# Feed-forward block on one core: the first chunk of x by DMA transposes instead of PE transposes

## Chip, cores and metric

The kernel runs on 1 core of one Trainium2 chip. The metric is the device time of one execution in microseconds (us), the median of several. The kernel before takes 94.9 us. All tensors are bf16, sums are fp32.

The profile names the engines PE (TensorE matmul), PEld (TensorE weight load), DVE (VectorE), ACT (ScalarE), POOL (GpSimd) and SP (SyncE). A name with a q (ACTq, SPq) is an engine's sequencer issuing DMAs. The granted clock is the share of TensorE's full clock that the profile says it was given. A DMA is issued by an engine, and it lands when its data has arrived and the semaphore says so; times of both are counted from the start of the profiled span.

## The reference

```python
# x: 1 x 2048 x 448, w1: 448 x 1792, w2: 1792 x 448
h = jnp.einsum("bsd,df->bsf", x, w1) + b1
h = gelu(h)                      # tanh approximation
return jnp.einsum("bsf,fd->bsd", h, w2) + b2
```

## The kernel before

The tokens are worked in four chunks of 512. Layer 1 needs x transposed (columns of x on the partitions, tokens along the row); 448 columns make three slots of 128 and one of 64. Each matmul uses 64 rows of the array where the dummy matmuls use 128 (forms 64\*128 and 128\*128 in the profile), and two of them, on the two row halves, run side by side: in the trace they start 3 to 4 ns apart. Such a pair is the unit of time: with 512 tokens the next one starts about 0.216 us later, and a chunk's layer 1 is 49 such pairs, 10.6 us. Two blocks of 128 hidden columns make an item, which holds one of four PSUM units.

How the first chunk gets in and is transposed:

```python
load_x()          # SyncE queue: xn[128 partitions, 4 tiles, 448], plain load, 448 KB
load_w1(0)        # 384 KB: hidden columns of items 0 and 1
load_w1r()        # 224 KB: the last 64 rows of w1
load_w1(1)        # 384 KB: items 2 and 3
load_w1(2)        # 576 KB
load_w2(0, 7); load_w2(7, 14); b2 ...          # 784 KB each
for c in range(1, NSC):                        # chunks 1 to 3: DMA transposes
    for slot, d0 in enumerate((0, P, 2 * P, D - P)):
        ... xT[:, slot, c*SC:(c+1)*SC] <- x2[c*SC:(c+1)*SC, d0:d0+P], transpose=True
# ... cut ...
warm(NWARM)       # 7 dummy matmuls of 512 columns, 0.43 us apart
for t, copier in enumerate(("vector", "scalar", "vector", "scalar")):
    ... turn(t, copier)       # PE transposes of one tile into PSUM, then one copy into xT
for c in range(NSC):
    items = [layer1(c, j) for j in range(2)]
    if c == 0:
        turn_b1() ...
        for t0 in (0, HC):                     # first half of the tokens, then the second
            for item in items:
                item[0](t0, t0 + HC)
    # ... cut: the other items, then layer 2 of the chunk ...
```

In layer 2 of the last chunk the last tile (`last=True`) adds its bias by a matmul, just before that tile's own matmuls:

```python
def part_a():
    need = free(u)                             # gelus that still read this PSUM unit
    if last:
        pr.op("tensor", ... matmul(unit[u][:, 1, 0:n], ones, b2_z ...), after=need + ["b2z"])
    # ... cut ...
```

Of the kernel before, what the change touches and what calls it, by code (L numbers as in the profile page):

```python
# [10 lines left out]

class Program:

# [3 lines left out]
    def __init__(self, nc, es):  # L17
        self.nc, self.es = nc, es
        self.lists = {e: [] for e in self.COMPUTE + ("sync",)}
        self.sems = {e: es.enter_context(nc.semaphore(f"sem_{e}")) for e in self.COMPUTE}  # L20
        self.count = dict.fromkeys(self.COMPUTE, 0)
        self.where = {}

    def op(self, engine, make, after=(), event=None):
        if event is not None:
            self.count[engine] += 1
            self.where[event] = (f"sem_{engine}", self.sems[engine], self.count[engine])
        self.lists[engine].append((make, tuple(after), self.sems[engine] if event else None, 1))

    def dma(self, engine, make, event, after=()):  # L30
        if event not in self.where:
            name = "dma_" + "_".join(str(p) for p in (event if isinstance(event, tuple) else (event,)))
            self.where[event] = (name, self.es.enter_context(self.nc.semaphore(name)), 0)
        name, sem, n = self.where[event]
        self.where[event] = (name, sem, n + 16)
        self.lists[engine].append((make, tuple(after), sem, 16))

    def barrier(self, engine, after):
        self.lists[engine].append((None, tuple(after), None, 0))

    def emit(self):
        for name in self.lists:
            self._run(getattr(self.nc, name), name)

    def _run(self, eng, name):
        seen = {}
        for make, after, sem, inc in self.lists[name]:
            for event in after:
                key, s, value = self.where[event]
                if seen.get(key, 0) < value:  # L50
                    eng.wait_ge(s, value)
                    seen[key] = value
            if make is None:
                continue
            done = make(eng)
            if sem is not None:
                done.then_inc(sem, inc)


def bass_standalone__dense_activation_gelu__prompt_kernel(  # L60
# [21 lines left out]
    NWARM = 7  # L82

    with ExitStack() as es:
# [5 lines left out]
        xn = sb("xn", [P, STC, D], BF16)  # L90
        xr = sb("xr", [P, STC, P], BF16)
        ident = sb("ident", [P, P], BF16)
        junk = sb("junk", [P, 1], BF16)
        b1n = sb("b1n", [P, P], BF16)
        b1_f = sb("b1_f", [P, NFT], FP32)
        b2_bc = sb("b2_bc", [P, D], BF16)
        g = sb("g", [P, NFT, S], BF16)
# [8 lines left out]
        x0v = x2[0:SC, :].rearrange("(p t) d -> p t d", t=STC)  # L106
        o0v = out2[0:SC, :].rearrange("(p t) d -> p t d", t=STC)


        W1CUTS = (0, 4, 8, 14)  # L110

        def load_x():
            pr.dma("sync", lambda e: e.dma_start(xn[:, :, :], x0v[:, :, :]), "x")  # L113
# [16 lines left out]
        load_x()  # L130
# [6 lines left out]
        pr.dma("sync", lambda e: e.dma_start(b2_bc[:, :], b2.partition_broadcast(P)), "b2")  # L137
        for c in range(1, NSC):
            for slot, d0 in enumerate((0, P, 2 * P, D - P)):
                pr.dma("sync", lambda e, c=c, slot=slot, d0=d0: e.dma_start(  # L140
                    xT[:, slot, c * SC:(c + 1) * SC], x2[c * SC:(c + 1) * SC, d0:d0 + P], transpose=True), ("xT", c))


        pr.op("gpsimd", lambda e: e.memset(ident[:, :], 0.0), event="ident0")
        pr.op("gpsimd", lambda e: e.affine_select(
            out=ident[:, :], in_=ident[:, :], compare_op=ALU.not_equal, fill=1.0,
            base=0, pattern=[[-1, P]], channel_multiplier=1), after=["ident0"], event="ident")
        pr.op("vector", lambda e: e.memset(b1n[:, :], 0.0), event="b1z")  # L148
        pr.dma("scalar", lambda e: e.dma_start(b1n[0:NFT, :], b1.rearrange("(c p) -> c p", p=P)), "b1n",
               after=["b1z"])  # L150
        pr.op("scalar", lambda e: e.activation(junk[:, :], one, ACT.Gelu_apprx_tanh))  # L151


        busy = {}
# [6 lines left out]
        def stage(t):  # L161
            return unit[t // 2][:, t % 2, 0:2 * P].bitcast(BF16)

        def twice(t):
            pr.op("vector", lambda e: e.tensor_copy(  # L165
                xr[:, t, :].rearrange("p (two h) -> p two h", two=2),
                xn[:, t, D3:D].unsqueeze(1).broadcast_to([P, 2, H])), after=["x"], event=("xr", t))

        def turn(t, copier):
            for k in range(KT + 1):  # L170
                src = xn[:, t, k * P:(k + 1) * P] if k < KT else xr[:, t, :]
                need = ["ident", "x"] if k < KT else [("xr", t)]
                pr.op("tensor", lambda e, k=k, src=src: e.transpose(  # L173
                    stage(t)[:, k * P:(k + 1) * P], src, ident[:, :]),
                    after=need, event=("xt", t) if k == KT else None)

            def evac(e):
                o = xT[:, :, t * P:(t + 1) * P]
                i = stage(t).rearrange("p (k s) -> p k s", k=KT + 1)
                return e.copy(o, i) if copier == "scalar" else e.tensor_copy(o, i)  # L180

            pr.op(copier, evac, after=[("xt", t)], event=("xT0", t))
            busy[(t // 2, t % 2)] = ("xT0", t)

        def turn_b1():
            b1T = unit[0][:, 1, 0:H].bitcast(BF16)
            pr.op("tensor", lambda e: e.transpose(b1T, b1n[:, :], ident[:, :]),
                  after=["b1n", "ident", ("xT0", 1)], event="b1T")
            pr.op("vector", lambda e: e.tensor_copy(b1_f[:, :], b1T[:, 0:NFT]), after=["b1T"], event="b1")
            busy[(0, 1)] = "b1"  # L190




        order = [2]
# [9 lines left out]
        serial = [0]  # L205

        def fence():
            serial[0] += 1
            return ("half", serial[0])

        def layer1(c, j):
            u = next_unit()
            c0, c1 = c * SC, (c + 1) * SC
            turned = fence()

            def mm(lo, half, k, t0, t1, first, fin, after, event):
                ft = 2 * j + lo
                rows = slice(half * H, (half + 1) * H)
                lhsT = w1_sb[rows, k, ft * P:(ft + 1) * P] if k < KT else w1r[rows, ft * P:(ft + 1) * P]
                pr.op("tensor", lambda e: e.matmul(  # L220
                    unit[u][:, lo, t0:t1], lhsT=lhsT, rhs=xT[rows, k, c0 + t0:c0 + t1], start=first, stop=fin,
                    skip_group_check=c == 0 and j < 2), after=after, event=event)

            def part_a(t0=0, t1=SC):

                need = free(u) if t0 == 0 else []
                need += [("xT0", t) for t in range(t0 // P, t1 // P)] if c == 0 else [("xT", c), ("xTd", c)]
                for k in range(KT):
                    for lo in (0, 1):
                        after = (need if k == 0 else []) + [("w1", w1_of(2 * j + lo))]  # L230
                        mm(lo, lo, k, t0, t1, k == 0 and t0 == 0, False, after,
                           turned if k == KT - 1 and lo and t1 == SC else None)

            def part_b():
                for k in range(KT + 1):
                    for lo in (0, 1):
                        fin = k == KT
                        mm(lo, 1 - lo, k, 0, SC, False, fin, [turned] if k == 0 else ["w1r", "w1rU"] if fin else [],
                           ("h", c, 2 * j + lo) if fin else None)
                for lo in (0, 1):  # L240
                    ft = 2 * j + lo
                    pr.op("scalar", lambda e, lo=lo, ft=ft: e.activation(  # L242
                        g[:, ft, c0:c1], unit[u][:, lo, :], ACT.Gelu_apprx_tanh,
# [3 lines left out]
            return part_a, part_b  # L247

        def store(c, st, after):
            j = c * STC + st  # L250
            dst = o0v[:, st, :] if c == 0 else out2[j * P:(j + 1) * P, :]
            pr.dma("sync", lambda e: e.dma_start(dst, out_sb[:, j, :]), "out", after=after)

        def layer2(c, tiles, last=False):

            u = next_unit()
            split = len(tiles) == 1
            n = DH if split else D
            turned = fence()

            def mm(ft, lo, half, first, fin, after, event):
                st = tiles[0] if split else tiles[lo]
                j = c * STC + st
                rows = slice(half * H, (half + 1) * H)
# [135 lines left out]
```

## Time and profile before

| | kernel before |
|---|---|
| median of 4 runs | 94.88 us (94.75 to 95.02) |
| profiled span | 93.5 us |
| PE busy | 90.2 us, 97% of the span |
| granted clock | 1.00 |
| first layer-1 matmul | 6.23 us |
| first layer-2 matmul | 16.83 us |

First, the chain of waits of the kernel before, followed back from its last instruction. Columns: start, length (us), what it was.

```profile
1.19 5.00 DMA w_sb<-in_w_dram
...
6.23 10.77 PE u L220 x110
17.00 10.59 PE u L266 x112
...
80.50 6.73 PE u L266 x85
...
```

One wait of 5 us for w1's first piece, then only matmuls to the end: L220 is layer 1, L266 layer 2. The first chunk's layer 1 (10.77) is hardly longer than a later one (10.58), so all that a better start can save lies before 6.23 us.

Second, the timeline of its start. Columns: start, length, engine, line, operation, out<-in, form, count, and in brackets the idle time before it and what ended it.

```profile
0.73 0.40 SPq L113 DMA_DIRECT2D xn<-in_x_dram  x1
1.19 0.42 SPq L120 DMA_DIRECT2D w_sb<-in_w_dram  x1
...
3.91 0.30 DVE L165 COPY xr<-xn 128x128 bf16<-128x128 bf16 x2 [2.98 <-DMA xn<-in_x_dram]
...
5.98 0.59 ACT L180 COPY xT<-u 128x512 bf16<-128x512 bf16 x1 [0.33 <-PE u L173]
...
6.23 2.13 PE L220 MATMUL u<-xT,w_sb 64*128 64x256 bf16 x30 [0.17 <-DMA w_sb<-in_w_dram]
```

x has landed by 3.9 us and is transposed and copied by 6.6; w1's first piece lands at 6.2. The two paths end nearly together.

Third, what the view of the tile xT says of the DMA transposes of chunks 1 to 3: issue time as min/median/max in ns, then the time from issue to landing.

```profile
L140 SPq DMA_TRANSPOSE xT<-in_x_dram x12: 1251/1262/2087, 9.2 to 25.5; - x12
...
DMA to landing us min/median/max: 3.0/4.0/6.0
```

All twelve have the same size, 512 tokens by 128 columns.

Fourth, the timeline where layer 1 of the last chunk ends:

```profile
79.68 2.42 ACT L242 ACTIVATE g<-u,b_f 128x512 bf16<-128x512 f32 x4 [0.24 <-PE u L220]
...
80.13 0.38 PE L220 MATMUL u<-xT,w1r 64*128 64x512 bf16 x2
...
80.34 6.89 PE L266 MATMUL u<-w_sb,g 64*128 64x448 bf16 x85
```

Layer 2 starts at 80.34 without a pause, while the last four gelus run until 82.1.

### The profile page before, as it was taken

The numbers are of one execution on the slowest core, as the hardware profiler recorded it, in microseconds if no ns is written. First come the engines' busy times: TensorE is split into PE (matmuls) and PEld (weight loads), VectorE is DVE, ScalarE is ACT, GpSimd is POOL, SyncE is SP. The second block draws the span as 40 slices with busy tenths as digits, with TensorE's granted clock in tenths as the row PEclk, the third lists the DMA queues.
The fourth block names the chain that finished last, engine by engine and source line by source line (L and its number), as shares of the span: only waits on it lengthen the run. The fifth ranks groups of instructions, "written<-read, shape, count | busy, mean of one in ns | idle before, by whom it ended". The sixth has DMA issues, their size and how long they took to land.

```text
span 93.5 us, 2049 instructions
## 1 busy us (share of the span) xinstructions
PE 90.2 (97%) x933; PEld 46.7 (50%) x933; DVE 12.3 (13%) x29; ACT 38.0 (41%) x61; POOL 1.1 (1%) x7
## 2 busy tenths in 40 slices
PE   6999999999999999999999999999999999999990
PEld 2475444555454444455554444455554444475890
DVE  0151001100334000000234000000134000000421
ACT  3353787900002887900001878900001878910001
POOL 4000000000000000000000000000000000000000
PEclk9999999999999999999999999999999999999999
DMA  2999999745665000000033000000033000000023
GB/s 51 324 224 365 379 328 126 136 94 113 64 128 173 0 0 0 7 0 0 0 102 101 0 0 0 4 7 0 0 98 98 0 7 0 0 0 7 17 81 98
DMA packets 12260, 7.32 MB, mean 78 GB/s; under 512 B 6940, under 2 KB 12060, under 8 KB 12252
## 3 DMA queue, kind: packets, MB, share of 16 engines
q1 hardware_dynamic: 12224, 7.20, 31.3%
q8 instruction: 7, 0.11, 0.5%
q10 hardware_dynamic: 28, 0.00, 0.0%
q14 instruction: 1, 0.01, 0.0%
HBM read 3.79 MB, written 1.84 MB: 60 GB/s over the span
## 4 chain that ended last, share of the span: by engine, by line
PE 91%; DMA 5%; SPq 0%; DVE 0%; issue 0%
PE u L266 46%; PE u L220 45%; DMA w_sb<-in_w_dram 5%; SPq L113 0%; DVE out_sb L305 0%; PE u L273 0%
## 5 line engine op out<-in xcount | busy, mean ns | idle before, releaser
L242 ACT ACTIVATE g<-u,b_f 128x512 bf16<-128x512 f32 x56 | 35.0, 686 | 40.5 <-PE u L220 40.5
L266 PE MATMUL u<-w_sb,g 64*128 64x448 bf16 (+1 forms) x504 | 43.2, 328 | 0.0
L220 PE MATMUL u<-xT,w_sb 64*128 64x512 bf16 (+1 forms) x348 | 40.9, 369 | 0.2 <-DMA w_sb<-in_w_dram 0.2
L266 PEld LDWEIGHTS u<-w_sb,g 64*128 64x128 bf16 x504 | 24.5, 94 | 18.4
L220 PEld LDWEIGHTS u<-xT,w_sb 64*128 64x128 bf16 x348 | 16.9, 94 | 19.3 <-DMA w_sb<-in_w_dram 0.5
L290 DVE TENSOR_TENSOR out_sb<-u,b_bc 128x448 bf16<-128x448 f32 x14 | 8.1, 620 | 61.2 <-PE u L266 61.2
L220 PE MATMUL u<-xT,w1r 64*128 64x512 bf16 x56 | 10.6, 376 | 0.0
L220 PEld LDWEIGHTS u<-xT,w1r 64*128 64x128 bf16 x56 | 2.7, 94 | 3.3
L308 ACT CAST out_sb<-u 128x224 bf16<-128x224 f32 x1 | 0.3, 346 | 9.2 <-PE u L266 9.2
L158 PE MATMUL u<-const-bfloat16-1.0 128*128 128x512 bf16 x7 | 3.1, 627 | 0.8 <-PEq L385 0.8
L180 ACT COPY xT<-u 128x512 bf16<-128x512 bf16 x2 | 1.2, 586 | 2.3 <-PE u L173 2.3
L158 PEld LDWEIGHTS u<-const-bfloat16-1.0 128*128 128x128 bf16 x7 | 0.9, 137 | 2.1 <-issue 2.1
L151 ACT ACT_TABLE_LOAD x1 | 1.3, 1283 | 1.6 <-DVE b1n L148 1.6
L173 PE MATMUL u<-ident,xn 128*128 128x128 bf16 x12 | 1.8, 308 | 0.1
L173 PEld LDWEIGHTS u<-ident,xn 128*128 128x128 bf16 x12 | 1.3, 138 | 1.0 <-issue 1.0
L361 DVE COPY xT<-xT 64x512 bf16<-64x512 bf16 x3 | 0.9, 289 | 3.5 <-DMA xT<-in_x_dram 3.4
L173 PE MATMUL u<-ident,xr 128*128 128x128 bf16 x4 | 1.2, 306 | 0.0
L357 DVE COPY b_z<-b_bc 1x448 bf16<-1x448 bf16 x1 | 0.3, 267 | 6.5 <-DMA b_bc<-in_b_dram 6.5
L165 DVE COPY xr<-xn 128x128 bf16<-128x128 bf16 x4 | 0.6, 190 | 3.0 <-DMA xn<-in_x_dram 3.0
L180 DVE COPY xT<-u 128x512 bf16<-128x512 bf16 x2 | 0.9, 426 | 0.7 <-PE u L173 0.7
L298 DVE TENSOR_TENSOR out_sb<-u,b_bc 128x448 bf16<-128x448 f32 x1 | 0.6, 625 | 1.7 <-PE u L266 1.7
L173 PEld LDWEIGHTS u<-ident,xr 128*128 128x128 bf16 x4 | 0.6, 138 | 0.1
(16 smaller groups left out, 3.4 us busy)
## 6 DMA issues: line engine op xcount, KB each, us to landing
out_dram<-out_sb SPq DMA_DIRECT2D x16, 112.0 KB, 1.7
w_sb<-in_w_dram SPq DMA_DIRECT2D x2, 784.0 KB, 9.3
w_sb<-in_w_dram SPq DMA_DIRECT2D x2, 384.0 KB, 5.5
w_sb<-in_w_dram SPq DMA_DIRECT2D x1, 576.0 KB, 6.9
xn<-in_x_dram SPq DMA_DIRECT2D x1, 448.0 KB, 3.2
w1r<-in_w_dram SPq DMA_DIRECT2D x1, 224.0 KB, 5.7
xT<-in_x_dram SPq DMA_TRANSPOSE x12, 4.0
b_bc<-in_b_dram SPq DMA_DIRECT2D x1, 112.0 KB, 9.1
```

The source lines that it names most:

```text
L151: pr.op("scalar", lambda e: e.activation(junk[:, :], one, ACT.Gelu_apprx_tanh))
L158: pr.op("tensor", lambda e: e.matmul(unit[3][:, 1, 0:cols], lhsT=ones_w, rhs=ones_m[:, 0:cols], start=True, stop=True))
L165: pr.op("vector", lambda e: e.tensor_copy(xr[:, t, :].rearrange("p (two h) -> p two h", two=2), xn[:, t, D3:D].unsqueeze(1).broadcast_to([ ...
L173: pr.op("tensor", lambda e, k=k, src=src: e.transpose(stage(t)[:, k * P:(k + 1) * P], src, ident[:, :]), after=need, event=("xt", t) if k ...
L180: return e.copy(o, i) if copier == "scalar" else e.tensor_copy(o, i)
L220: pr.op("tensor", lambda e: e.matmul(unit[u][:, lo, t0:t1], lhsT=lhsT, rhs=xT[rows, k, c0 + t0:c0 + t1], start=first, stop=fin, skip_group ...
L242: pr.op("scalar", lambda e, lo=lo, ft=ft: e.activation(g[:, ft, c0:c1], unit[u][:, lo, :], ACT.Gelu_apprx_tanh, bias=b1_f[:, ft:ft + 1], s ...
L266: pr.op("tensor", lambda e: e.matmul(unit[u][:, lo, 0:n], lhsT=g[rows, ft, j * P:(j + 1) * P], rhs=w2_sb[rows, ft, d0:d0 + n], start=first ...
L290: pr.op("vector", lambda e, lo=lo, j=j: e.tensor_tensor(out=out_sb[:, j, :], in0=unit[u][:, lo, 0:D], in1=b2_bc[:, :], op=ALU.add), after= ...
L298: pr.op("vector", lambda e: e.tensor_tensor(out=out_sb[:, j, :].rearrange("p (two h) -> p two h", two=2), in0=unit[u][:, :, 0:DH], in1=b2_ ...
L308: pr.op("scalar", lambda e: e.copy(out_sb[:, j, DH:D], unit[u][:, 1, 0:DH]), after=[("y", c, tiles[0], 1)], event=("o", j, 1))
L361: pr.op("vector", lambda e, cs=cs: e.tensor_copy(xT[0:H, KT, cs], xT[H:P, KT, cs]), after=[("xT", c + 1)], event=("xTd", c + 1))
```

## The change

The intent: no PE transposes, no copies out of PSUM, and no x load ahead of w1. x of the first chunk comes already transposed by eight DMA transposes of 256 tokens, on ScalarE's otherwise idle queue, and layer 1 begins with the first slot of the first 256 tokens. The core of the diff (the rest rewrites bookkeeping: waits between matmuls are derived automatically, b1 comes by GpSimd's queue and is transposed by DVE, layer 2's matmuls are reordered; cut):

```diff
-        load_x()
+        def load_xT(engine, s0, s1, slot, event, after=()): ...   # one DMA transpose
         load_w1(0)
         load_w1r()
         # ... cut: the other weights, unchanged ...
+        for h in (0, 1):
+            for slot in range(KT + 1):
+                load_xT("scalar", h * HC, (h + 1) * HC, slot, ("x0", h, slot))
+        first_x = [("x0", h, slot) for h in (0, 1) for slot in range(KT + 1)]
         for c in range(1, NSC):
-            ... transposes on the SyncE queue
+            ... the same, but the first of them waits for first_x
-        warm(NWARM)                      # 7
-        for t, copier in enumerate(...): ... turn(t, copier)
+        warm(NWARM)                      # 6
+        for k in range(KT):
+            for i in (0, 1):
+                items[i].step("a", k, 0, HC)
+            warm(1, HC)
+        items[0].b(0, HC)
+        items[1].b(0, HC)
+        items[2].a(0, HC)
+        items[0].a(HC, SC)
+        items[1].a(HC, SC)
+        items[2].b(0, HC)
+        items[0].b(HC, SC)
         # ... cut ...
+                q, r = Layer2(c, (2,)), Layer2(c, (3,), True)
+                r.bias()                 # the bias matmul, now ahead of the last layer 2
+                p.part("a", every)
```

The wait on `first_x` keeps the two queues' streams of transposes from being in flight together (ScalarE's last one lands at 16.45 us, SyncE's first is issued at 16.53).

## The prediction

> **What bounds the kernel now.** TensorE. The page shows PE busy 97% of the 93.5 us span; the chain of waits is 5.0 us of waiting for the first w1 piece (issued at 1.19, landed 6.19 us), then matmuls without a gap from 6.23 to 91.3 us. By pieces of the chain, layer 1 takes 10.77 us for chunk 0 (ending at 17.00) and 10.58 us for each later chunk, layer 2 takes 10.59 us. Chunks 1 to 3 cannot gain.
>
> **What the change does.** It removes the PE transposes, their evacuations and the 448 KB x load that lies ahead of w1 in SyncE's queue. It adds eight 256-token DMA transposes on ScalarE's queue, cuts three pairs of chunk 0's layer 1 into halves of 256 tokens, reorders layer 2 and moves the last tile's bias matmul ahead of the last layer 2.
>
> **Costs.** Now, a 512-token transpose issues in 1.25 us and lands 3.0 us after issue at best, 4.0 in the median (the xT tile's view). Estimate for 256 tokens: 0.65 us to issue, landing 2.4 us after issue undisturbed. Slot 0 of the first half then lands at about 3.5 to 4, the eighth transpose at 8 to 9.5. Transpose packets are 256 B and take about 20 ns (trace's DMA records): 2,048 of them are 2.6 us of all 16 engines, where the x load took 128 packets of about 147 ns, 1.2 us. [...] the transposes compete with w1 during the very time when w1 is critical; the trace shows the engines already over 90% busy from 2 us on.
>
> **Critical path.** Work in chunk 0 is 10.57 us; what counts is each arrival plus the work that can only follow it. w1's first piece now lands about 4.7: the first matmul starts 1.5 us earlier. But w1r plus its copy (7.84 now) has 9.6 us of work after it, w1's second piece (8.2 now, about 8.4 after) has 9.06 us, the second half's first slots 8.5 us, its last slot with copy 7.3 us. So w1's second piece sets the end of chunk 0's layer 1 at about 17.4, not 17.0: the early start turns into waits inside chunk 0. ScalarE has issued by 6 to 7 us and loaded its table by 8.5; that should not bind.
>
> **A new loss at the end.** The last tile's bias matmul needs the PSUM unit of pair 5 of chunk 3. Before, the four last gelus start at 79.68 and the second ends at about 80.95, while PE is ready at 80.3. PE is in order, so about 0.6 us is lost.
>
> Sum: 94.9 + 0.4 + 0.6 = 95.9 us; range 94.1 to 97.6. Faster by over 2%: 4%; within 2%: 74%; slower: 22%.
>
> **What would show it.** First layer-1 matmul near 4.7; PE waits for DMA of w1r/w1 or xT in 5 to 9 us, 1 to 2 us in total; first layer-2 matmul at about 17.4; a wait of about 0.6 us for a ScalarE gelu ahead of the bias matmul; stages between at 10.58.
>
> **What would make it wrong.** The transposes overlap w1's inefficient phase (about 230 GB/s from 5 to 7 us now) and cost it nothing: chunk 0 ends near 16, total 94.4. Or they get a small share beside the weights, the second half lands after 10 us, or the gaps keep the matmul clock at its starting rate (warm-up matmuls 0.43 us apart, against 0.215 later): 97 and more.

## The result, and the profile after

The changed kernel is correct and much slower. Ratios here are the mean time of one kernel's fast runs over that of the other's of the same rounds, so not quite the ratio of the medians.

| | before | after |
|---|---|---|
| median, 4 runs each | 94.88 us | 104.89 us (103.36 to 105.27) |
| ratio of fast runs | | 1.0965 (95%: 1.0839 to 1.1092) |
| profiled span | 93.5 us | 103.7 us |
| PE busy | 97% | 90% |
| first layer-1 matmul | 6.23 us | 6.63 us |
| first layer-2 matmul | 16.83 us | 26.35 us |

The changed kernel varies by several per cent from run to run. The run of its profile counts as slow by the rule (over 1.5% above its fastest run), at an unlowered granted clock of 1.00.

The chain of waits after:

```profile
0.73 1.20 ACTq L141
...
7.68 1.27 ACTq L141
...
8.98 6.84 DMA xT<-in_x_dram
...
15.86 73.34 PE u L202 x724
89.20 1.26 ACT g L253 x2
...
90.60 10.96 PE u L202 x169
...
```

The chain begins with issuing: six transposes, one after the other, until 8.95; the seventh, issued at 8.98, lands at 15.82. Only then do the matmuls run through. Near the end a gelu stands in the chain, which was not there before.

The timeline after, at the places that answer to those of before (L202 is now the line of all real matmuls):

```profile
0.73 10.88 ACTq L141 DMA_TRANSPOSE xT<-in_x_dram  x8
...
6.63 0.61 PE L202 MATMUL u<-xT,w_sb 64*128 64x256 bf16 x4 [3.13 <-DMA xT<-in_x_dram]
...
8.85 0.61 PE L202 MATMUL u<-xT,w_sb 64*128 64x256 bf16 x4 [1.29 <-DMA xT<-in_x_dram]
...
10.66 0.61 PE L202 MATMUL u<-xT,w_sb 64*128 64x256 bf16 x4 [0.88 <-DMA xT<-in_x_dram]
...
15.86 1.68 PE L202 MATMUL u<-xT,w_sb 64*128 64x256 bf16 x14 [0.99 <-DMA xT<-in_x_dram]
...
26.35 3.94 PE L202 MATMUL u<-w_sb,g 64*128 64x448 bf16 x40
```

Each slot starts a burst of four matmuls, then PE waits for the next slot. By the trace's semaphore records the eight slots land at 6.5, 8.8, 10.6, 11.8, 13.0, 14.4, 15.8 and 16.4 us. The weights are early: w1's first piece is there at 4.1, w1r at 5.6, w1's second piece at 7.6 (before: 6.2, 7.4 and 8.2).

The view of the tile xT in the first 17 us:

```profile
L202 PE MATMUL u<-xT,w_sb x46: 368/417/418, 6.6 to 16.9; 64*128 64x256 bf16 x46
L141 ACTq DMA_TRANSPOSE xT<-in_x_dram x8: 1197/1303/1499, 0.7 to 10.3; - x8
...
DMA to landing us min/median/max: 2.6/6.8/7.2
```

A transpose of 256 tokens takes as long to issue as one of 512 did, 1.3 us, and 6.8 us to land. The matmuls of 256 tokens take 417 ns here; the same form takes 269 ns in the kernel before.

The end of the last layer 1 after:

```profile
89.19 2.42 ACT L253 ACTIVATE g<-u,b_f 128x512 bf16<-128x512 f32 x4 [0.24 <-PE u L202]
...
89.64 0.38 PE L202 MATMUL u<-xT,w1r 64*128 64x512 bf16 x2
...
90.60 0.25 PE L202 MATMUL u<-b_z,const-bfloat16-1.0 64*128 64x224 bf16 x1 [0.58 <-ACT g L253]
```

PE stands for 0.58 us before the bias matmul, waiting for a gelu. From the last pair of layer 1 to layer 2 it now takes 0.96 us (89.64 to 90.60), where it took 0.21 (80.13 to 80.34).

So of the 10.2 us that the span grew, 9.5 came before the first layer-2 matmul (26.35 against 16.83), and 0.7 at the end.

### The profile page after: what moved, and what is told of

Read it like the earlier page. It is cut to its first block, busy times and chain, and to the rows that moved or that the text cites. A ratio compares the mean times of both kernels' runs of the same rounds, so it can differ in the third digit from the quotient of the medians.

```text
span 103.7 us, 2084 instructions
## 1 busy us (share of the span) xinstructions
PE 93.9 (90%) x948; PEld 49.3 (48%) x948; DVE 12.1 (12%) x29; ACT 36.7 (35%) x59; POOL 1.3 (1%) x6
## 4 chain that ended last, share of the span: by engine, by line
PE 81%; ACTq 8%; DMA 7%; ACT 1%; issue 0%; DVE 0%
PE u L202 81%; ACTq L141 8%; DMA xT<-in_x_dram 7%; ACT g L253 1%; DVE out_sb L310 0%
## 5 line engine op out<-in xcount | busy, mean ns | idle before, releaser
L202 PE MATMUL u<-xT,w_sb 64*128 64x512 bf16 (+1 forms) x372 | 45.9, 381 | 6.3 <-DMA xT<-in_x_dram 6.3
L202 PE MATMUL u<-w_sb,g 64*128 64x448 bf16 (+1 forms) x504 | 43.2, 328 | 0.0
L202 PEld LDWEIGHTS u<-w_sb,g 64*128 64x128 bf16 x504 | 26.2, 94 | 16.4
L202 PEld LDWEIGHTS u<-xT,w_sb 64*128 64x128 bf16 x372 | 19.0, 101 | 27.7 <-DMA xT<-in_x_dram 4.4
L202 PE MATMUL u<-xT,w1r 64*128 64x512 bf16 (+1 forms) x62 | 12.2, 377 | 0.0
L202 PEld LDWEIGHTS u<-xT,w1r 64*128 64x128 bf16 x62 | 3.5, 102 | 3.7 <-DVE w1r L321 0.4
L177 PE MATMUL u<-const-bfloat16-1.0 128*128 128x512 bf16 (+1 forms) x9 | 3.9, 548 | 0.8 <-PEq L393 0.8
L172 DVE COPY xT<-xT 64x512 bf16<-64x512 bf16 (+1 forms) x5 | 1.3, 263 | 17.6 <-DMA xT<-in_x_dram 17.5
L166 DVE STREAM_TRANSPOSE b1t<-b1n 32x32 bf16<-32x32 bf16 x4 | 0.8, 202 | 4.0 <-DMA b1n<-in_b_dram 3.9
L202 PE MATMUL u<-b_z,const-bfloat16-1.0 64*128 64x224 bf16 x1 | 0.3, 252 | 0.6 <-ACT g L253 0.6
L163 POOL DMA_DIRECT2D b1n<-in_b_dram x1 | 0.6, 632 | 0.1
L202 PEld LDWEIGHTS u<-b_z,const-bfloat16-1.0 64*128 64x128 bf16 x1 | 0.1, 92 | 1.1 <-ACT g L253 1.1
L162 POOL MEMSET b_z<- 128x448 bf16 x1 | 0.5, 472 | 0.3 <-POOLq L393 0.3
## 6 DMA issues: line engine op xcount, KB each, us to landing
b_bc<-in_b_dram SPq DMA_DIRECT2D x1, 112.0 KB, 11.8
```

What stands on the lines that cost most here:

```text
L162: pr.op("gpsimd", lambda e: e.memset(b2_z[:, :], 0.0), event="b2z0")
L163: pr.dma("gpsimd", lambda e: e.dma_start(b1n[0:NFT, :], b1.rearrange("(c p) -> c p", p=P)), "b1n", after=["b1z"])
L166: pr.op("vector", lambda e, q=q: e.transpose(b1t[32 * q:32 * q + 32, :], b1n[:, 32 * q:32 * q + 32]), after=["b1n"], event=("b1t", q))
L172: pr.op("vector", lambda e: e.tensor_copy(xT[0:H, KT, s0:s1], xT[H:P, KT, s0:s1]), after=after, event=event)
L177: pr.op("tensor", lambda e: e.matmul(unit[3][:, 1, 0:cols], lhsT=ones_w, rhs=ones_m[:, 0:cols], start=True, stop=True))
L202: o = pr.op("tensor", lambda e: e.matmul(unit[u][:, lo, cols], lhsT=lhsT, rhs=rhs, start=start, stop=stop, skip_group_check=skip), after=a ...
```

## The experiments

My theory after the result had two parts: a transpose costs about 1.3 us of issue whatever its size ("per instruction"), and the clock of TensorE had dropped while it waited. The main rival was "bytes": beside the weights the transposes' bytes get too little of the DMA engines.

| run | the change with | median us (before in the same rounds) | ratio | last x slot, us | layer 1 of chunk 0 ends, us |
|---|---|---|---|---|---|
| | nothing else | 104.89 (94.88) | 1.0965 | 16.4 | 26.35 |
| e1 | four transposes of 512 | 105.02 (94.83) | 1.1074 | 14.1 | 25.90 |
| e2 | w2, b2 after x | 101.69 (94.83) | 1.0736 | 12.3 | 22.81 |
| e3 | dummies in the gaps | 104.39 (94.83) | 1.0995 | 16.5 | 26.08 |
| e9 | fewer dummies | 103.86 (94.72) | 1.0983 | 17.1 | 25.08 |
| e5 | e1, and all from w1's third piece held; bias late | 98.56 (94.60) | 1.0368 | 8.9 | 20.45 |
| e6 | e5, and w1's second piece held | 98.44 (94.60) | 1.0386 | 7.7 | 20.36 |
| e10 | e5 with dummies | 98.26 (94.72) | 1.0389 | 9.6 | 20.56 |
| e12 | nothing else, again | 104.95 (94.81) | 1.0837 | 16.1 | 25.81 |

The ends are those of each run's one profile, the medians those of all its runs. Slots are from the trace's semaphore records.

### e4: what a transpose costs by itself

The kernel before, with pairs of transposes into scratch after its last store, first on SyncE's queue, then on ScalarE's:

```diff
+        for eng in ("sync", "scalar"):
+            # two each of 128, 256, 512 and 1024 tokens by 128 columns, each size after the last has landed
+            pr.dma(eng, lambda e, ...: e.dma_start(t[:, 0:n], x2[0:n, 0:P], transpose=True), ("p", i), prev)
```

> The kernel before, with 16 transposes into scratch after its last store: pairs of 128, 256, 512 and 1024 tokens by 128 columns, first on SyncE's queue, then on ScalarE's, nothing else on the DMA engines. 'Per instruction': issue takes about 1.25 us for 128, 256 and 512 alike on both queues. My prediction's estimate: in proportion to tokens, 0.3, 0.65, 1.25, 2.5. A third idea: ScalarE's queue is simply twice as slow as SyncE's, 0.65 for 256 tokens on SyncE and 1.3 on ScalarE. The kernel's own part is not changed; the time is longer by the probe, 25 to 35 us.

Correct; 126.66 us with the probe, one run, state unknown, so only the times of the transposes themselves count. The view of the scratch tile; L376, L379, L382 and L385 are 128, 256, 512 and 1024 tokens, and the three numbers are min/median/max in ns:

```profile
L376 SPq DMA_TRANSPOSE probe<-in_x_dram x2: 1101/1164/1227, 93.4 to 94.6; - x2
L379 SPq DMA_TRANSPOSE probe<-in_x_dram x2: 1104/1173/1242, 96.9 to 98.1; - x2
...
L385 SPq DMA_TRANSPOSE probe<-in_x_dram x2: 1161/1230/1298, 104.4 to 105.6; - x2
L376 ACTq DMA_TRANSPOSE probe<-in_x_dram x2: 1169/1212/1255, 109.3 to 110.5; - x2
L379 ACTq DMA_TRANSPOSE probe<-in_x_dram x2: 1120/1196/1273, 112.9 to 114.1; - x2
...
L385 ACTq DMA_TRANSPOSE probe<-in_x_dram x2: 1177/1254/1331, 120.5 to 121.7; - x2
```

Eight times the tokens cost 6% more issue time, and the two queues differ by about 4% at most. My estimate of 0.65 us for 256 tokens is refuted, and so is a slower ScalarE queue. Eight transposes need about 10 us of issuing. With nothing beside them the transposes of 256 tokens landed 2.3 to 2.4 us after issue: 1.1 to 1.3 of issuing, 0.1 until the first packet, 0.5 to 0.6 of packets and 0.5 from the last packet to the landing.

### e1: half as many transposes, the same bytes

```diff
-        for h in (0, 1):
-            for slot in range(KT + 1):
-                load_xT("scalar", h * HC, (h + 1) * HC, slot, ("x0", h, slot))
+        for slot in range(KT + 1):
+            load_xT("scalar", 0, SC, slot, ("x0", slot))
```

> The first chunk's x comes by four transposes of 512 tokens instead of eight of 256, same queue, same bytes, weights untouched. Theory 'per instruction' (a transpose costs about 1.3 us of issue whatever its size, and they proceed one per issue): issuing ends at about 6 us instead of 11.6, the last slot lands near 12 instead of 16.4, chunk 0's layer 1 ends near 23.5 instead of 26.3, time near 102. Rival 'bytes' (the transposes' 512 KB get a small share of the DMA engines beside the weights): the last bytes land at about 16.4 as before, and since all work now waits for whole slots, layer 1 of chunk 0 ends at 26 to 28 and the time is 105 to 107.

105.02 us, no gain. The timeline shows that the issuing is indeed over early, and that it did not help:

```profile
0.73 5.58 ACTq L141 DMA_TRANSPOSE xT<-in_x_dram  x4
...
10.53 0.61 PE L201 MATMUL u<-xT,w_sb 64*128 64x256 bf16 x4 [2.97 <-DMA xT<-in_x_dram]
...
12.39 0.61 PE L201 MATMUL u<-xT,w_sb 64*128 64x256 bf16 x4 [0.93 <-DMA xT<-in_x_dram]
```

All issued by 6.3, yet the second slot is there only at 10.5 and the last at 14.1. "Per instruction" alone had said 12 for the last slot and 102 us, and fails. "Bytes" had said 16.4 for it, which fails too, though its 105 to 107 us for the time held: fewer instructions did bring the last slot forward, by 2.4 us. They also brought the first half's last slot back, from 11.8 to 14.1, since each slot is now twice as large. The two cancel.

The trace's DMA records show the sharing. Packets started in half a microsecond; x packets are 256 B, w2 packets 896 B. These are counts of the records, not a view:

```
run and window (us)                  x packets               w2 packets
e1, five, from 10.77 to 13.27        151 127 155 156 164     156 160 154 153 150
after, three, from 9.27 to 10.77     103 108 116             140 137 118
e5, 6.27 to 6.77, weights almost in  515                   none (2 of w1)
```

With both queues full, about one x packet starts for each w2 packet in four of e1's five windows (151 to 164 against 150 to 156). The order of the records in e1's windows says the same: 816 starts of w2 packets lie 4 ns before the end of an x packet, against 95 to 280 at each of the other lags looked at (from 6 ns before to 12 after), and starts of x packets show no such peak (at most 300). The changed kernel's trace has the same peak from 8.5 to 15 us: 1,367 at 4 ns before, 306 to 545 at each other lag from 8 ns before to 13 after, and at most 402 for starts of x packets. So most x packets are followed by a w2 packet and not by another x packet. One for one is a bad bargain for the queue with the small packets: 155 packets of 256 B in 0.5 us are 79 GB/s for x in e1, where the same transposes reach 264 GB/s in e5 (515 packets) with the engines nearly to themselves. The prediction counted the transposes' packets, but not what share beside the weights they would get.

### e2: the later weights wait for x

```diff
         def load_w2(a, b):
             pr.dma("sync", lambda e: e.dma_start(
-                w2_sb[:, a:b, :], ...), ("w2", a))
+                w2_sb[:, a:b, :], ...), ("w2", a), first_x)      # b2 is issued behind them
```

> w2 and b2 are issued only when the first chunk of x has landed; the eight transposes are untouched. 'Per instruction': issuing still takes 1.2 to 1.5 us each, so the eighth is issued at 10.3 and lands not before 13; spacing of landings stays 1.3 us, only the lag from issue to landing (6.8 us in the changed kernel) falls to about 3; chunk 0's layer 1 ends near 23, time near 102. 'Bytes': as soon as w1 is in (about 9 us) the waiting transposes rush in, several within 1 us, and the lag rather than the issue was the limit: the first half lands by 9 and the second close behind its issue. A third idea, 'one line' [...]: the lag is short from the second transpose on, also while w1 is still coming in.

101.69 us, 3.3 us better than e1 in the same rounds. The timeline:

```profile
0.73 10.45 ACTq L141 DMA_TRANSPOSE xT<-in_x_dram  x8
...
9.62 0.61 PE L203 MATMUL u<-xT,w_sb 64*128 64x256 bf16 x4 [2.40 <-DMA xT<-in_x_dram]
...
22.81 5.46 PE L203 MATMUL u<-w_sb,g 64*128 64x448 bf16 x56
```

The slots land at 6.5, 9.6, 9.9, 10.2, 10.4, 11.1, 11.5 and 12.3. As soon as w1's last piece is in (9.4 us), four come within 0.8 us: until then the weights were the limit. The last two slots land 2.9 and 2.4 us after their issue (the eighth is issued at 9.9), with their first packets 0.1 us after the issuing ends, as in e4: from then on the issuing is the limit. Both causes are real, one after the other. "One line" (x waits behind SyncE's w2 and b2) fails in its simple form, since the second slot, issued at 1.96, still took until 9.6.

### e5 and e6: both levers

```diff
 # e5: e1's diff, and
+        pr.barrier("sync", first_x)       # SyncE waits for all of x
         load_w1(2)                        # e6: the barrier stands ahead of load_w1(1)
 # NWARM = 12; r.bias() back behind p.part("b", every)
```

> Both levers at once: four transposes of 512 tokens, and everything after w1's second piece (w1's third, w2, b2) issued only when x has landed; also the bias matmul back in its late place and 12 warm-up matmuls. Issuing ends at about 6 us. If weights in the other queue hold the transposes up ('sharing'), only w1's first two pieces and w1r can do so now, and they are in by 7.7: the four slots land by 8.5 to 9.5, chunk 0's layer 1 ends at 19 to 19.5, the bias stall is gone, and the time is 96.5 to 98. If the delay belongs to the transposes themselves (they lag 6 us behind issue whatever runs beside), the last lands at 11 or later and the time stays above 99.

98.56 us; slots at 6.1, 7.9, 8.5 and 8.9. The arrivals are as "sharing" said. The end of layer 1 is 1 us later than expected; the matmuls after the last slot again run slowly at first, a pair of 256 tokens in about 0.21 us from 9.59 to 11.27 (see e3).

> As the run before it, but w1's second piece is held too, so that only w1's first piece and w1r run beside the four transposes. Sharing: the four slots land at the pace of issue, 1.25 us apart, the last at 7.3 to 8.0. Then w1's second piece is issued at about 8 and lands at about 10.3, with 9 us of work behind it: chunk 0's layer 1 ends at about 19.5, time 97 to 98.5, no better than the run before. If the delay belongs to the transposes themselves, the last slot lands at 10 or later and the time is 100 or more. Either way I expect more than the 94.9 of the kernel before: four issues and a landing alone take longer than its x load, PE transposes and evacuation (6.6 us).

98.44 us; slots at 6.6, 7.0, 7.3 and 7.7. The last falls in its range, but the pace does not: the slots land 0.3 to 0.4 us apart and not 1.25, since the first, issued at 0.73, took until 6.6 even here. The time is in its range. The chain of waits of e6 shows what takes their place:

```profile
4.74 2.96 DMA xT<-in_x_dram
...
7.79 3.42 DMA w_sb<-in_w_dram
...
11.25 83.59 PE u L202 x911
```

Now w1's second piece comes at 11.2, 0.9 us later than I had estimated, and is what layer 1 waits for. The last slot of the same four transposes came at 14.1 (e1), 8.9 (e5) and 7.7 us (e6), the less weight traffic was left beside them, the earlier. But holding weights back only moves the wait from x to w1.

### e3, e9 and e10: the clock

e3 fills the gaps with dummy matmuls: 18 ahead of the first slot, 8, 7, 1 and 4 between the steps of the first half, 4 and 5 between those of the second:

```diff
-    NWARM = 6
+    NWARM = 18
-            warm(1, HC)
-        items[0].b(0, HC)
+            warm((8, 7, 1)[k])
+        for k in range(KT):
+            items[0].step("b", k, 0, HC)
+        warm(4)
+        items[0].step("b", KT, 0, HC)
-        items[0].a(HC, SC)
-        items[1].a(HC, SC)
+        for k in range(KT):
+            for i in (0, 1):
+                items[i].step("a", k, HC, SC)
+            warm((4, 5, 0)[k])
```

> The changed kernel with idle TensorE time of the first 16 us filled with dummy matmuls (18 at the start, 4 to 8 in each wait for an x slot). Theory 'cold clock': after 15.86 us the changed kernel ran pairs of 256-token matmuls in about 0.24 us instead of 0.11 for some 4 us, and lost 2 us by it; with the gaps filled they run at 0.11 and the time falls by 1.5 to 2 us, to about 103. Rival (the slow stretch comes from the 256-token halves or their fences, not from the clock): the stretch stays slow and the time stays at 104.8 or rises by the dummies' overshoot of up to 0.5.

104.39 us, not told apart from 104.9. But the rate is as the theory says. The timeline of the changed kernel after its last long wait, and then that of e3:

```profile
15.86 1.68 PE L202 MATMUL u<-xT,w_sb 64*128 64x256 bf16 x14 [0.99 <-DMA xT<-in_x_dram]
17.33 0.42 PE L202 MATMUL u<-xT,w1r 64*128 64x256 bf16 x2
```

```profile
17.74 0.72 PE L202 MATMUL u<-xT,w_sb 64*128 64x256 bf16 x10
18.29 0.27 PE L202 MATMUL u<-xT,w1r 64*128 64x256 bf16 x2
```

In the changed kernel 14 matmuls take 1.47 us to the next group, 0.21 for a pair; in e3 10 take 0.55, 0.11 for a pair. In e3 the work from there to layer 2 takes 8.34 us (17.74 to 26.08); in the changed kernel 10.49 us (15.86 to 26.35), of which about 0.2 us is work that e3's order had done already. So the slow clock costs about 2 us. e3 did not earn it, because its last dummies ran on for over 1 us after the slots had come.

The clock records show two rates, full and half, and the pairs keep to them: 0.11 and 0.21 us. e5's record has half clock for 3.41 us, from 8.01 on. The changed kernel's trace has no clock record before 19.83 us, where full clock begins; the six dummies at its start (0.43 us apart; e3's come 0.21 apart from about 4.1 us on) and its pairs until then (0.21 us from 11.7 us on) run at half rate. So in that run the clock had not dropped in the waits, as my theory had it: it had not yet risen. The page's row of the granted clock prints 9 where there is no record, and so reads full speed through the slow stretch. In e2, with the same six dummies, the record has full clock from 4.16, half from 7.58, in the wait before the second slot, and full again from 14.40; why it rose early in e2 and not in the changed kernel is not shown:

```profile
PEclk9995569999999999999999999999999999999999
```

e9 is e3 with 17 dummies at the start, then 8, 4 and 2, then 2 and 4.

> As e3_warm_fill, but with fewer dummies late, since there the last ones ran on for 1 us after the slots they waited for had landed. If the cold clock costs 2 us, chunk 0's layer 1 now takes 8.4 us from the third slot of the second half (at about 15.9 to 16.2) and ends at 24.3 to 24.8, and the time is 102.8 to 103.3; if the gain of e3 was chance, it stays at 104.9.

103.86 us, 0.6 above the range. The work after the third slot again took 8.34 us (16.74 to 25.08), but in this profile that slot landed at 16.7 instead of 15.8. The rate is shown; a saving of 2 us in the time is not, because x's arrival differs by about that from run to run.

e10 is e5 with dummies (16 at the start, then 6, 2 and 2 between the slots):

> As e5_hold_from_w1_2 (four transposes of 512 tokens, w1's third piece, w2 and b2 after x, bias late), with dummy matmuls in the gaps of 6.5 to 9.6 us. If the cold clock is the rest of its loss, pairs of 256-token matmuls take 0.11 from 9.6 on and the time falls by about 1 us to 97.4 to 97.7. It should still not beat the kernel before: the last slot lands at about 9 and 9.6 us of work follow it.

98.26 us, above the range of 97.4 to 97.7: a miss. All pairs of its profile run at 0.11, but the slots landed 0.3 to 0.7 us later than in e5 and the dummies ran on after them, so layer 1 ended at 20.56 against 20.45.

### e7: the bias matmul alone

The kernel before, with the bias matmul ahead of the last chunk's layer 2:

```diff
-                roll(layer2(c, (0, 1)))
-                roll(layer2(c, (2,)))
-                roll(layer2(c, (3,), True))
+                last3 = [layer2(c, (0, 1)), layer2(c, (2,)), layer2(c, (3,), True)]
+                last3[2][2]()               # the bias matmul
+                for item in last3:
+                    roll(item)
```

> The kernel before, with one part of the change alone: the last tile's bias matmul ahead of the last layer 2. Theory: it waits for the gelus of pair 5, TensorE is in order, so 0.6 to 0.7 us is lost: 95.5. Rival: the wait hides behind work in flight and nothing changes: 94.85.

95.69 us against 94.60, ratio 1.0103 (1.0064 to 1.0143). Its chain of waits has the new link:

```profile
69.99 9.76 PE u L220 x90
79.75 1.27 ACT g L242 x2
...
81.15 0.25 PE u L271
81.40 10.71 PE u L266 x168
```

The gap is real: PE idles 0.58 us before the bias matmul, and layer 2 starts 0.96 us after the last pair of layer 1 instead of 0.21, so this profile lost 0.75 us there. The ratio's 1.0% is about 1.0 us (0.6 to 1.4), where I had expected 0.6 to 0.7. The bias's PSUM unit is still read by the gelus of item 5, and everything behind the bias in PE's order waits with it: layer 2's first matmul starts at 81.16, the bias at 81.15.

### e8 and e11: two tries at the kernel before

e8 brings b1 through GpSimd's queue and transposes it on DVE, as the change does. e11 issues w1's first piece on ScalarE's queue beside x.

```diff
 # e8
-        pr.dma("scalar", ... b1n ...)        # and a PE transpose
+        pr.dma("gpsimd", ... b1n ...)        # and four DVE transposes of 32 x 32
 # e11
-            pr.dma("sync", ... w1 piece i ...)
+            pr.dma("scalar" if i == 0 else "sync", ... w1 piece i ...)
```

> The kernel before, with another part of the change alone: b1 comes through GpSimd's queue and is transposed by VectorE, not by a PE transpose. In the kernel before the first layer-1 matmul waits for the last of the sixteen shares of w1's first piece, which came at 6.2 us, 0.9 us after the fifteenth-latest shares; b1's small DMA is in flight just ahead of it. If b1's DMA delays that straggler, layer 1 starts at 5.7 to 5.9 and the time is 94.4; if not, the start stays at 6.2 and the time at 94.85, within 0.1.

95.16 us, ratio 1.0029 (0.9985 to 1.0074): nothing shown. In its profile w1's first piece landed at 6.6, so moving b1 to another queue does not bring it forward. Whether b1's DMA delays the straggling share (in the kernel before, 6.19 us where the other fifteen are in by 5.33) is not shown: it was still in flight here too, and landed at 6.8.

> The kernel before, with w1's first piece on ScalarE's queue beside x on SyncE's, instead of behind it. If its late landing (6.2 us) comes from standing behind x, layer 1 starts at 5.7 to 6.0 and the time is 94.4 to 94.6; if the two only share the engines, x lands later by what w1 gains and the time stays within 0.3 of the kernel before, in either direction.

95.98 us median, with three of six runs slow; ratio of fast runs 1.0073 (1.0030 to 1.0116), slightly slower, by more than the 0.3 us allowed for. w1's first piece lands at 5.9 instead of 6.2, but x at 4.4 instead of 3.9, and the PE transposes after it decide.

### e12: the changed kernel once more

No edit.

> The changed kernel itself, unedited, once more, since its first profile fell in a run that the rule calls slow (over 1.5% above the fastest of the same kernel, at an unlowered granted clock). If my account holds for its faster runs too, a profile of a fast run shows the same order of events: weights early, x slots 1.2 us apart with the third of the second half at 15 to 16 us, a stretch of matmuls at half rate after it, layer 1 of chunk 0 ending at 25 to 26.3, a stall of 0.6 us ahead of the bias matmul. If the loss were a thing of the slow run, layer 1 of chunk 0 would end before 22.

104.95 us median of 6 (102.75 to 107.97), ratio 1.0837 (1.0741 to 1.0934). The profiled run was again slow (104.52), so it shows that the order of events repeats: issues 1.2 to 1.4 us apart, the seventh slot at 15.1, the end of layer 1 at 25.81, the wait before the bias. A profile of a fast run of this very kernel I don't have; the fast profiles of e1, e3 and e9 show the same.

## Why the prediction was wrong

**What held.** TensorE bounds the kernel before (busy 97% of the span), and a change there can only touch the start and the end. The stall before the bias was predicted at 0.6 us and is 0.58 us of idle PE, 0.7 with the overlap lost; e7 shows it alone, at 1.0% of the time. The change did lose where I said it would, in waits inside chunk 0.

**The step that failed** is the arrival of x: "Estimate for 256 tokens: 0.65 us to issue, landing 2.4 us after issue undisturbed", and from it "the eighth transpose at 8 to 9.5". It is wrong in two terms.

- Issue: 1.2 to 1.5 us each (e4: 1.16 us for 128 tokens, 1.23 for 1024, on SyncE), so the eighth is issued at 10.3, not at 5.3 (0.73 and seven times 0.65). I halved a duration that I knew at one size only. The trace had a hint: the plain loads of 224 to 448 KB at the head of the queue were issued in 0.40 to 0.55 us, not in proportion to their bytes.
- Landing: 6.8 us after issue in the median. The undisturbed figure was right (2.3 to 2.4 us for 256 tokens in e4), the allowance for the weights beside it was not. I assumed that the transposes compete with the weights, but let the weights pay for it ("w1's second piece ... about 8.4 after"). It landed at 7.6, earlier than before, and x paid. e1, e5 and e6 show this with the same four transposes: 14.1, 8.9, 7.7 us as weights are taken away. In the changed kernel's packet records the delay has two parts. The third slot's first packet starts 3.4 us after its issuing ended (0.1 in e4). From then on, 8.26 to 15.71, the packets of the last six slots follow one another almost without a break, about 103 in half a microsecond; at e5's 515 the same 1,536 would need 1.5 us (my estimate) instead of 7.5. The first slot failed too: estimated at 3.5 to 4, it landed at 6.5, so layer 1 began at 6.63 and not near 4.7.

So "w1's second piece sets the end of chunk 0's layer 1 at about 17.4" fell. The third slot of the second half sets it: it lands at 15.8, its matmuls start at 15.86, and about 8.5 us of work at full clock (10.57 less 19 pairs of 256 tokens at 0.108, which precede it) would end at 24.4. The remaining 2 us is the half rate until 19.83 (pairs at 0.21 us, in e3 0.11). Together: 7.5 (x) + 2.0 (clock) + 0.7 (bias) = 10.2, the whole growth of the span.

The prediction did name both causes among what would make it wrong ("they get a small share beside the weights", "the gaps keep the matmul clock at its starting rate"), at "97 and more", and the second is just what the trace shows (dummies 0.43 us apart, pairs at 0.21 us until full clock begins at 19.83). It gave slower by over 2% only 22%, and treated them as alternatives. They come as a chain: late slots make the gaps, and after the gaps the changed kernel, e1, e2 and e5 work for a while at 0.21 us a pair (e3 and e9, with more dummies at the start and in the gaps, at 0.11).

**What stays open.** Why the second and third transposes put no packet on the engines for about 1.6 and 3.4 us after their issuing had ended, while weights were flowing (in e2 no x packet starts between 7.0 and 7.9, with the third one issued by 4.7), is not settled: one packet for one does not explain silence. With w1's second piece held too, the second transpose's packets began at 5.1 (e6) instead of 5.6, most of them only after 6.2 (e5). Nor is it settled why the first slot landed 2.6 us after its last packet had started (0.5 in e4). The 1.2 to 1.4 us between slots beside w2 is what 256 packets take at the pace counted above; why that pace was about 103 in half a microsecond where e1 reached 151 to 164 in four of its five windows is open. Not tried: the transposes on SyncE's queue, among the weights in one order.

**No better kernel was found.** Even repaired, the DMA route loses: four issues and a landing put the last slot at 7.7 at the earliest (e6), and w1 had to wait for it. The kernel before has x transposed at 6.6 while its weights flow.

## What to carry to other kernels

Before cutting a DMA into smaller ones for an earlier start, measure its cost at two sizes: a DMA transpose cost its issuing engine about 1.2 us at every size from 128 to 1024 tokens (e4). Where two queues load at the same time, count packets and not bytes alone: in e1 a stream of 256 B packets got 79 GB/s beside one of 896 B packets, where e5 reached 264 GB/s without it. Here what was needed first was the stream of small packets beside bulk loads, and its last slot came at 16.4 us. And the early waits of TensorE cost twice here, once as waits and once as 2 us of work at half clock after them (0.21 us a pair instead of 0.11). And a matmul placed early must not need a buffer that is still being read: e7's bias matmul held PE for 0.58 us, and the matmuls behind it with it.
